# A merged issue list, dealt buffer places and five idle products in a spectral and GLU kernel

## The chip, the cores and the metric

The kernel runs on one core of one Trainium2 chip. The time is device microseconds of one execution. Three executions of the kernel before took 1094.29, 1090.46 and 1092.93 us; their median is 1092.93 us. Engines are named as in the profile: PE multiplies matrices, DVE, ACT and POOL work on vectors, SP issues DMAs (POOL and ACT issue some too).

## The reference

Four layers act in turn on x of 2048 rows and 512 columns, in fp32. A is a filter in the spectrum, B is a bilinear gated unit; each works on the normalised x and is added to x.

```python
def _A_ref(x, w_r, w_i):
    X = jnp.fft.rfft2(x, axes=(-2, -1))
    X = X * (w_r + 1j * w_i)
    return jnp.fft.irfft2(X, s=(S, D), axes=(-2, -1))

def _B_ref(x, w_gate, w_up, w_down):     # 512 -> 1792 -> 512
    h = (x @ w_gate) * (x @ w_up)
    return h @ w_down

x = A_x
x = x + _A_ref(_layernorm(x), A_w_r, A_w_i)
x = x + _B_ref(_layernorm(x), B_w_gate, B_w_up, B_w_down)
x = x + _A_ref(_layernorm(x), A_w_r, A_w_i)
x = x + _B_ref(_layernorm(x), B_w_gate, B_w_up, B_w_down)
```

The output is x after the four.

## The kernel before, in words

**Tiling and stages.** x lives in SBUF as `xs`, 16 tiles of 128 rows by 512. The kernel calls an A with the B behind it a layer; there are two, and each runs through these stages.

- *Forward*, 16 tiles t (`fwd`, `fwd_rest`): statistics of the row, a scale by the reciprocal deviation put into a twiddle factor `tw`, for some tiles a fold `fo` on POOL, four products into a bank `tp` ("spread"), and copies or sums into `E`, which holds the spectrum.
- *Middle*, 16 groups g (`middle`): sums `fs` on DVE for g = 0 and 1 and on POOL for the others, sixteen small products into `dp` ("features"), a copy `zs` on ACT, a product `zp` by the constant `midt`, the filter on DVE into `ys`, products into `vq`, and a copy back into `E`. The first group needs all 16 forward tiles.
- *Inverse*, tiles t (`inv`): products `yi`, a copy or sum `vs`, a product `yo`, added to `xs`; then the statistics for B. Half the tiles run here, the other half between the first units.
- *Transposes* (`build_x`, and for the second half of the tiles `stage_x` and `unstage_x` through memory, with `zt`): the normalised tile `xn` is turned (`tq`) and split in a high and a low part, `XA` and `XS`.
- *Units* (`unit`): seven products of blocks (`gw`, `gx`, `gy`, `gz`, `gv`) with sums on DVE (`q`, `q5`, `c22`) and a copy `s1` on ACT in between, so that the gate and up products take seven instead of eight block products. The names s, q and c in the profile are `s1`, `q` or `q5`, and `c22`. Then the down products: plain (`db`) for the first and the last, in between in seven products again (`down`: `ex` to `ev`), whose left sides `sf` are made by ACT and POOL and whose right sides `bf` are fetched from memory by a DMA that POOL issues (`load_forms`). Every product of fp32 numbers is three products of fp32r parts (`mm3`).

**The order of the work.** Nothing is issued when it is written down. Each step is recorded by `plan.op` with its engine, what it reads (`r`) and what it writes (`w`); from these follow the steps that must stand before it. `Plan.order` then reads a list written into the kernel, `ORDER`: the compressed differences of the step numbers, 4939 of them. The steps are issued in that order, and `Queue.call` keeps every engine's instructions in program order, so the list sets the order on each engine. That call is line 296, and so all lines of the profile carry L296; its groups are told apart by their tiles.

**Rings.** Most tiles take a place in a ring, a set of buffers of one size: `x`, `y`, `w` (one bank of PSUM each), `a` (three), `d` (two), `f` (eleven of 128 by 512 in SBUF), and smaller ones for twiddles, statistics and the forms `sf`. `bank` and `temp` ask for a tile with the ring's name as its tag and the ring's size as its number of buffers, and the framework deals the place. A new tile waits until the last instruction that uses the former tile of its place has ended. For the forms (`slot`) `order` works out the place itself, as the one that was free for longest.

**At the start of each middle stage**, the last spreads, their copies into `E`, the first `fs` and the first features follow one another; in layer 0 that is near 27 us, in layer 1 near 573 us.

Of the kernel before, what the change touches and what calls it, by code (L numbers as in the profile page):

```python
# [11 lines left out]
F32 = mybir.dt.float32  # L12
# [16 lines left out]
def consts():  # L29
# [74 lines left out]
FAST = (0, 1)  # L104
FAHEAD, BOFF, COFF, IOFF, W1, HPDUE, TOFF = 2.79, 9.0, 6.0, 5.0, 10.0, 40.0, 6.0
# [29 lines left out]
    'Q`oVGf<F#0a$Q(2!7I(Mb2mHuDtXPx|Nq+=+9sGswG~nMmRQA-uYGh8_cnyOV3OL(Ch0%m&xv8hrO;<BgBM)DPkS`dD_k$<Iz{fI!nt4(2JdCEGSmXOZ~(Qz19B5Bx{@hh=GR)e6kjBZ'
    '>B_(98)(~D8&WaNMSDk~Mi@tgT}$0&zg`dOdoiB5pZ3{UXLV&m-6!@TzQEf?sm=B0v@!jY%nn~6FX82tSX~NbIXSF;oK&P%n;mRFq7TU%?ALQ*S?q#Z?OBQ)8zb+^&H6gE<3ReE8ng=K'
    'Bi7c7$QUG_f&8cO$fe}#++g1|SRVxxd=E;B$?bj7I5+d%pL_QbQH}^)tWETFv>aY#tm$&r-_Nf|CZMa5<VSj$RbF4F#pA^8bauNiU?No#dpS`jNh{d!xu7rx1S=vL2JTy;e>dp_btt>f'
    'sZ^beCy)1~K5?kJf-v${YKW_XI<U&?a$PKK^kVlF3Oa&aB9v8uHVXbUjWIvy&Qip2d9>eUpwCG!)?<D=K}?%PpZE-Cp2^imgLhMCS-@H%IZt+PNj~fV7gg3=(3%vYzj;{4#YE>4l)a7d'
    'c)0U=P$pI{JxjiPg3kbuHD5RBSysD^-V4Z5E#T1wp#CRcS=tgqsnQ$YZKG{s+!gvADsd7hnj?2IdWJ0XWATXX-wHK7pY5AEQyGTj0#@ciBn=4q^*dJeIr|%-j7<4=W>1d5rklcwEAqRK'
    'JPA9T;CD4@GS$gcZ0)el5Z5v==~(=0nz1E)pE8w3z4d^5(%&qmi6*1Go~QTc<n)2AIsWR6*9+l=F6hf=c)EyHu2j>aUEthD*_S@j)W7IVIh+N5U$Y9s$Uthu0$3<3>|83=7*<M$$Y{;3'  # L140
    'tt7v!)t*lM1+C@g_#W~Tb2RgBxw0X4o+aw4h7*qKSW|oXHYj{UN$KE|eBz=EHRSG4`|i-^X>UI22ygW8-(veteOz{iTs^~?5=tm4v(3Dbgoms6_E80_-bsCF9P=3Yxns11{Ff6vpAN6R'
    'MIWzQ8T&E*F2`GuWcr5DH?aIRyzg0;ja3LrpP_Cwm3ev4k#?el{$r(Aur}i%W8=l_N=<h3O8iradq3hYL-RcLuNRS15YE<mp_1(c;g?YB=7$rWoqXGA9GN&SA9Vns^VM+EiCw)8TwI3+'
    'JrK8#`pF0JIjt78#ClupXRP4c_<oeiAXsN>Si1)UUCD#Su_;(TkKQ}+Xz7GvgE{KJ7>D(f_~z(8@z`h^_tLnxgTEEn=^X4_5<iL>t4D9Iuf%<$h4Fx>JQ1>0n+ML0;H@WgkItokVouA{'
    'wR!ech{bE*jmP3?(IGXhvIHCriOVKUB<nZFht<eu4aj-F=;!!m11OI1$~?UYU)udlJ~csXS+T2#h%LZ_j_(|PH7&^-KfsN7VYUXW^N8LZuVu$=uh-Eki<$O;<r-pVhbvrHe?sepr^(cC'
    'J(zJdYQa?Q5!ysxcpKJL3~Hiz(2s@S#H)Q<2LBBm{v8NBfrUG$DJ?FKf!!*>nnF!vvKk?_?ToZmH~~Bz@Ysks8neGAiIIfjE)P4{&fB?XKNuql_j?mzso{*a4tX`3zX#PcR(jw&J10DZ'
    'uhuZuAAG9e$=b3^t(L67NOt0NnErLbcM(Xhf~DnY`w#TtNo<`52cHDNCt>?F`htwmcVMQ&L{B=SX0Xl*0SD>)U61zd#Yi_0ojWygV)h9r8$k~{yX(N}4ro)j_5dTNgXX3vigfxf)60S`'
# [54 lines left out]
class Plan:  # L201
# [36 lines left out]
    def order(self):  # L238
# [5 lines left out]
        for o in ops:  # L244
            for t in o["tiles"]:
                t.left, t.slot = t.users, None
# [21 lines left out]
def kernel(ctx: ExitStack, tc: tile.TileContext, x, wf, wc, wb, dfwd, tf, ti, mid, out):  # L268
# [679 lines left out]
    ws = {}  # L948
# [167 lines left out]
```

## Time and profile before

| | |
|---|---|
| median of three executions | 1092.93 us |
| the profiled execution | 1092.97 us |
| its span, first to last instruction | 1091.2 us |
| mean granted clock of PE | 0.991 |
| PE busy | 1059.6 us (97%), 6536 products |
| DVE busy | 817.0 us (75%) |
| POOL busy | 752.8 us (69%) |
| ACT busy | 404.2 us (37%) |

The table has the profiled execution beside the median of the others. Busy times are sums over the span; the rest of an engine's span is idle. PE is the engine that is seldom idle, so what matters is where it waits, and how fast it is allowed to run: the granted clock is 1.00 for nearly all of the span and 0.50 in a few stretches. In the timeline, a row has the start, the duration, the engine, the operation with its tiles (output, then inputs), the shape and the count; the bracket at its end is the time for which the engine was idle before it, and the instruction that ended that time. In the windows, each engine has its busy time and a count of instructions in brackets, and PEclk is the clock that was granted to PE.

### The profile page before, as it was taken

How to read it: one execution, taken by the hardware profiler on the slowest of the kernel's cores; microseconds unless marked ns; L12 is line 12 of the kernel's file. 1: busy time of each engine (PE TensorE's matmuls, PEld its weight loads, DVE VectorE, ACT ScalarE, POOL GpSimd, SP SyncE). 2: the span in 40 equal slices, each digit the busy share in tenths (PEclk: the TensorE clock that was granted, in tenths of full speed). 3: DMA queues.
4: the chain of work that ended last, by engine and by line, in shares of the span. 5: the costliest groups of instructions: out<-in, count | busy, mean ns of one | idle time of the engine just before them, and what ended most of it. 6: DMA issues, size and time to landing. Idle time of an engine off the chain costs nothing.

```text
span 1091.2 us, 18622 instructions
## 1 busy us (share of the span) xinstructions
PE 1059.6 (97%) x6536; PEld 912.2 (84%) x6536; DVE 817.0 (75%) x1603; ACT 404.2 (37%) x965; POOL 752.8 (69%) x1000
## 2 busy tenths in 40 slices
PE   8999999999899999999989999999999999999998
PEld 6676888888699988889976679888889998888887
DVE  7776867778777567777896768768888876667688
ACT  6456643333343322232354466123233422222321
POOL 6746698998899746757746328465578984656772
PEclk9999999999999999999998999999999999999999
DMA  9512545778663566547381001646778247555642
GB/s 354 222 44 108 173 174 202 244 243 284 191 218 139 203 202 205 182 149 229 123 323 71 1 18 58 213 153 194 224 241 261 78 138 245 187 189 195 206 135 78
DMA packets 84668, 193.65 MB, mean 177 GB/s; under 512 B 39264, under 2 KB 50784, under 8 KB 73568
## 3 DMA queue, kind: packets, MB, share of 16 engines
q0 software_dynamic: 16128, 102.77, 28.4%
q1 hardware_dynamic: 68160, 89.18, 24.3%
q8 instruction: 52, 0.85, 0.3%
q10 hardware_dynamic: 288, 0.52, 0.1%
q14 instruction: 40, 0.33, 0.1%
HBM read 145.52 MB, written 46.92 MB: 176 GB/s over the span
## 4 chain that ended last, share of the span: by engine, by line
PE 81%; DVE 7%; POOL 5%; ACT 2%; issue 1%; DMA 1%; DVEq 0%; POOLq 0%; ACTq 0%
PE gz L296 13%; PE gx L296 13%; PE gy L296 6%; PE gw L296 6%; PE gv L296 6%; PE db L296 6%; PE ex L296 5%; PE ez L296 5%; PE dp L296 3%; PE zp L296 3%; PE ew L296 3%; PE ey L296 3%; PE ev L296 2%; PE yi L296 2%; DVE xs L296 2%; PE vq L296 2%
## 5 line engine op out<-in xcount | busy, mean ns | idle before, releaser
L296 PE MATMUL gx<-xA,wt 128*128 128x512 f32 (+1 forms) x852 | 181.9, 349 | 4.1 <-ACT s L296 2.6
L296 PEld LDWEIGHTS gx<-xA,wt 128*128 128x128 f32 x852 | 138.3, 191 | 23.3 <-ACT s L296 3.2
L296 POOL TENSOR_TENSOR sf<-cc,sf 128x256 fp32r<-128x256 f32 x97 | 71.5, 739 | 48.6 <-ACT sf L296 47.3
L296 DVE TENSOR_TENSOR xs<-xs,db 128x512 f32<-128x512 f32 x128 | 85.1, 680 | 20.1 <-PE db L296 19.7
L296 POOL TENSOR_TENSOR sf<-q,sf 128x256 fp32r<-128x256 f32 x101 | 74.3, 739 | 34.5 <-ACT sf L296 31.0
L296 PE MATMUL db<-wd,h 128*128 128x512 f32 x336 | 91.6, 399 | 0.6 <-DVE xA L296 0.6
L296 PE MATMUL gy<-xS,wt 128*128 128x512 f32 (+1 forms) x426 | 90.7, 348 | 1.2 <-ACT xS L296 0.6
L296 PE MATMUL gz<-xA,wt 128*128 128x512 f32 (+1 forms) x426 | 90.7, 349 | 0.2 <-DVE c L296 0.2
L296 PE MATMUL gz<-xS,wt 128*128 128x512 f32 (+1 forms) x426 | 89.8, 347 | 0.7 <-DVE q L296 0.7
L296 PE MATMUL gv<-xS,wt 128*128 128x512 f32 (+1 forms) x426 | 90.0, 347 | 0.0
L296 PE MATMUL gw<-xS,wt 128*128 128x512 f32 (+1 forms) x426 | 89.9, 347 | 0.0
L296 ACT COPY s<-gx 128x512 f32<-128x512 f32 (+1 forms) x71 | 35.1, 495 | 144.2 <-PE gx L296 131.1
L296 PEld LDWEIGHTS gy<-xS,wt 128*128 128x128 f32 x426 | 69.0, 190 | 11.0 <-POOL xS L296 0.9
L296 PEld LDWEIGHTS gw<-xS,wt 128*128 128x128 f32 x426 | 69.4, 190 | 10.1 <-DVE q L296 0.4
L296 PEld LDWEIGHTS gz<-xS,wt 128*128 128x128 f32 x426 | 68.9, 190 | 10.3 <-DVE q L296 1.1
L296 PEld LDWEIGHTS gz<-xA,wt 128*128 128x128 f32 x426 | 68.8, 190 | 10.3 <-DVE c L296 0.9
L296 PEld LDWEIGHTS gv<-xS,wt 128*128 128x128 f32 x426 | 68.9, 190 | 9.3 <-issue 0.5
L296 POOL TENSOR_TENSOR wt<-rg,wt 128x512 fp32r<-128x512 f32 (+1 forms) x56 | 64.0, 1154 | 13.9 <-ACT wt L296 13.8
L296 PEld LDWEIGHTS db<-wd,h 128*128 128x128 f32 x336 | 61.4, 189 | 14.3 <-issue 3.2
L296 DVE TENSOR_TENSOR q<-gy,s 128x512 f32<-128x512 f32 (+1 forms) x71 | 40.9, 577 | 39.2 <-PE gy L296 23.4
L296 ACT CAST sf<-q 128x256 fp32r<-128x256 f32 x101 | 40.8, 406 | 72.5 <-DVE q L296 31.6
L296 PE MATMUL ex<-bf,sf 128*128 128x256 f32 x408 | 60.4, 285 | 1.2 <-DMA bf<-dn 1.2
(161 smaller groups left out, 2532.4 us busy)
## 6 DMA issues: line engine op xcount, KB each, us to landing
wt<-gu POOLq DMA_DIRECT2D x36, 1024.0 KB, 5.4
wt<-gu POOLq DMA_DIRECT2D x36, 768.0 KB, 5.1
bf<-dn POOLq DMA_DIRECT2D x20, 1024.0 KB, 5.5
wq<-in_wf_dram SPq DMA_DIRECT2D x16, 1024.0 KB, 10.9
bf<-dn POOLq DMA_DIRECT2D x20, 768.0 KB, 4.7
gu<-wt SPq DMA_DIRECT2D x14, 1024.0 KB, 5.8
gu<-wt SPq DMA_DIRECT2D x14, 768.0 KB, 5.1
rg<-in_wb_dram SPq DMA_DIRECT2D x14, 512.0 KB, 4.2
```

Source lines behind the costliest of these rows:

```text
L296: ins = f(*args, **kw)
```

## The change

- `ORDER` is a new list of 4944 steps. It was merged in order of the times that are expected for the steps.
- Every place of a ring is now a buffer of its own: its tag is the ring's name and a digit, and it has one buffer. The digit is read from a string, `PLACES`, which has 2328 hexadecimal digits, one for each tile in a ring in the order in which the list first uses them. The rings keep their sizes. `order` no longer works out any place.
- `keep_warm` records idle products ahead of the middle stage: two in layer 0, three in layer 1. Each is one product of 128 by 512 of the constant `midt` with itself into a new tile `wp` in bank `w`, which nothing reads. The key `"idle"`, written by the spread of the last tile (t = 15) and by the idle products and by the first features (g = 0), puts them in this order: last spread, idle products, first features.

```diff
+IDLE = 2, 3
 ORDER = (
-    ...
+    ...
+PLACES = (
+    ...
@@ class Tile_
-        self.users = self.left = 0
-        self.freed = 0.0
+        self.users, self.placed = 0, False
         self.index = 0
         self.tile = None
+
+    def tag(self):
+        return f"{self.ring}{self.index}"
@@ Plan.order
-        ops, rings, done = self.ops, {}, set()
-        turn = np.cumsum(steps.astype(int))
+        ops, done = self.ops, set()
+        turn, places = np.cumsum(steps.astype(int)), iter("".join(PLACES))
         assert sorted(turn) == list(range(len(ops)))
-        for o in ops:
-            for t in o["tiles"]:
-                t.left, t.slot = t.users, None
-        for n, i in enumerate(turn):
-            o = ops[i]
-            assert o["pre"] <= done
+        for i in turn:
+            assert ops[i]["pre"] <= done
             done.add(int(i))
-            for t in o["tiles"]:
-                if t.slot is None:
-                    t.slot = True
-                    q = rings.setdefault(t.ring, [])
-                    t.index = len(q)
-                    if len(q) == self.RINGS.get(t.ring, 1):
-                        old = min((u for u in q if not u.left), key=lambda u: u.freed)
-                        t.index = old.index
-                        q.remove(old)
-                    q.append(t)
-            for t in o["tiles"]:
-                t.left -= 1
-                t.freed = n
+            for t in ops[i]["tiles"]:
+                if not t.placed:
+                    t.placed, t.index = True, int(next(places), 16)
         return [ops[i] for i in turn]
@@ bank, temp
-        return Tile_(name, tag, lambda: pp.tile([128, 512], F32, name=name, tag=tag, bufs=NB[tag]))
+        t = Tile_(name, tag, lambda: pp.tile([128, 512], F32, name=name, tag=t.tag(), bufs=1))
+        return t
...
-        return Tile_(name, tag, lambda: wk.tile(list(shape), dt, name=name, tag=tag, bufs=NB.get(tag, 1)))
+        t = Tile_(name, tag, lambda: wk.tile(list(shape), dt, name=name, tag=t.tag(), bufs=1))
+        return t
@@ fwd_rest
-        pe(0.9, spread, [*src, tw], [tp])
+        pe(0.9, spread, [*src, tw], [tp, *(["idle"] if t == 15 else [])])
@@
+    def keep_warm(n):
+        for i in range(n):
+            bk = bank("wp", "w")
+            pe(0.86, lambda bk=bk: TE.matmul(bk(), midt[:, 0:128], midt, start=True, stop=True), ["midt"], [bk, "idle"])
@@ middle
-        pe(0.83, features, [(fs, 0), (fs, 1), df], [dp])
+        pe(0.83, features, [(fs, 0), (fs, 1), df, *(["idle"] if g == 0 else [])], [dp])
@@ the loop over the layers
         dcs["i"] = load_di()
+        keep_warm(IDLE[layer])
         for g in range(16):
             middle(g, E, dcs["f"], W, t0 + BOFF + BSTEP * g, SWAPS[layer][g])
```

More of the change, by code (lines that the diff above doesn't have):

```diff
@@ new lines @@
+    '<w4$>uES&(y^7Ogofg5*g##b%WS$pfk+xv$!#rQCCuIUriY8(gS!;1gWt0j*|Ie}Ts=go#iF%4YBXgOlIUXs@O8UuC?JH{;VYrTvjy!u=RxwXanWJ-cy!_2ti{jZF;!=@VMDpGkd=Vy-'
+    'S$_>?36n|siMVy$(~-Pgk$6?aKT)z%XW*^k@`^6`*Q)YZenTBf?r8$H4AFU#$=H!nOnT^ixrQB~c)tWFzoyOcVHnSgGor&=CUzH<r-)C4xE@_}C#~r^P*+HaAR`J&3tc9qiDV9|GxD@t'
+    'u?n&-N_|<bO>|e#k|E`_h$$+q%`bi_bJdnITlGo2(+k{&%MwuDM3(8Jyb~@N_JVvW&thQ>y&y^EjIAeA)W^>~<qx8mLBE<>*rejgNkk(~zQ^Wr8fKCiGZ_yK2HPF+)D$pVPE(0@x`xO;'
+    '(9%^_fSY|}nUQB$wdxw($JkA!EODzZZ*$#3R-15}U(;m1OtM*;VBD(S)B^mjNe12LtqRy4g3S@c`W$Fz#MR^AEmk(^er;@`^fI=j5&=)1k`F+7L+KzRwHi;FV|BJplr?1JYcfq+;{SK`'
@@ new lines @@
+    'aXBMH^j)6r!h0UMmQTh=6+BU%(N&Xmi5`bjX6hh$p1dC;N!s6hX)noE)>xUgu~M1$zR@=DLsPCQgQtV?8Ch(}=`&=;dELdEugWm#6WmpzR~UHjOHTE{mO0v$XwT7ab%Tr{_Yd-O1O#jY'
+    'eMfYUz62^3X?ND%m-oI0+dFi-Ow<u(t(^&0j65OxOkdkiJ^^j{WwQ>I!#Y}KgXDTxGMo|f%h&Qce05Z}>QgYs%hF5}$@XlWjtyl&*H^53xJ+dY<;cj%`ig0%9hk8=a~fi*<Wr1%N|xS%'
+    'Nfz49W}jZQCCnWn@<76|B1`W3L^gkz-@vbIdJvg@QVf16C@Ogx31i)cqjEub1YRh{xOZ6jcM^luj?avom6D+B3|Emnzol2DxZaS8MAM^h7*8U}n=IP8!M>-Zs>JJJo;Q@Gj8ei}v5{sE'
+    'mKGs4`QSYxe@Y{A%~ciAl4dUvOC`_Kh{0JcqGioFdRKNe2VM*}S$dYaDye7AXay`PB!}@u8JMw}oaV`Ma?0j6=WQi(-=@I$?svFekxF><7@63V9F8X!Lb3fZ*rlua7^XO7|1yQN9HaDQ'
@@ new lines @@
+    '-Fx7}IiT-vJxv}S#d~R5MIXVo8q}OhuxpAw3-=t*npz7xLiILW(i}9jBr+#qoK$;I`hwnB+8@83wDnCMqf}yLw|Npx#QxMFAmDdab{GG<igAg|{L)5><-H1W+;%X|C+juS_AwXmK}Bjw'
+    'EKj!K8CTCzK!=gpww!587NoP9J#h4LZ7Zd~%rff5cKf<Hs=LXkY2YkB78Qki7wI#2?=lsk8M9v33mQkfvg|GT*E8@OSH(2MC?oE(*O{v}<1fP7x%fYqoV$RBp2K%Zc&Rze(@lP6<rcdP'
+    '4E{8|e_}<u$=n#K_bmEUk?*vXB!c(H$=@_$l>wrv!9LGY^=8<eW)Ys)3U6)29s>&1dh)V4#a##DdWH(Kff~AtIm$6=y8gus>D;C9-exk}p(395&d|1*k$c*`W)-z8m0av;J@3PyPg6XT'
+    'tqtwRW|Tc^uEWcPseBh<fkzp2AwD{!pV=Qxe)uq54^q(w;O|a$nz^NKS-8bqgfpIH?Hz51cMjg^0?Qra_ph`X-uW9(_mUict?6Lrk?{q*ba=0uElBSNx&x-T1drC%*QLG9F@KY7b-`sc'
@@ new lines @@
+    'N-2$OZ7*f*2@_-Ud3XJB*qo32S;uNDKTdU2mUKTy&zU6ZSy^!zlI45MTTp6wtMwJT&BPOr$`WNSnzMc@$tPc#o)YQ3?oYKLjPSl`%{m{Uwmi(SlOX-H-_6_0OegetZ@zz&6||COGMe$@'
+    '!G0V_9c1sB^?o-wXEu@%b3x5~oe8EQ><IIL6k_Dz=9hp+7s6B{sWWGE7I>c^tNb)A?IlPxnc?Sh^&F$k)KBFLKi*66U-Rbrjl501k(a%1{d`_?d~+VOu7qp$Q^(3;mD7P|u=NaROvZ!F'
+    'si&L#1TT$Bwafp=d&4j0J@9LI#iSGHS}Co}CI2pMW4UW8seTOeT-Wm^Ru1}K(A$&t-a2OV^>c59=C?bvmFMBN4`qzsT<+o7vHr8(CI6yH_q%&>GRq(2z3or-R9Aw(^ZL8r&#Ob`Uf^zl'
+    '-@|)Vn)z*|9b-m$7ySy}FaD=^`z!CD{^T34f$i@l!&p^hp6{}`rX+atSo;J2r1tWT`D)^b;WJW4+WYIg(>g~##O@dIevC9lH@5McvXXYeyVJZO{H=x#7~{RJ1?(X2XPto6(O!y%+dREz'
@@ new lines @@
+    's>%ibhQ8p1VVMEx9lVv~XiK!sRs5O{Zk!#|yT<Y>ez{MC8j$(vT3_Dv-}8!siZy;`R$?{AJL@<0+K}I&sEBR4-k;zZkn;nT=^&Wdh0PuC<xsB*b^o%S$7eNQfyPwW7s>GXy3k+g{RL+|'
+    'VCJe=f13FdsdO>YLVh83Jx$%bS>9G{jV?Y(o<_n<7hw37@N=Z>hpA)HPP@T!X*i)aSj>PYQv(()LpA&ZJ#vmdam2*!368_+u`sq9v7|idU)DulG`>2)Xr%%zRgO$*#pqFTk&KOF#!Rqv'
+    '0F;!$%BzfA3R}vN+a1Iy^)ghY0$lkh^V`%sMIlFt``Ls2+oU=fa)r5%gUsL6mo|*BQQYpp*Qa4upX#(yp44#PdMBxbUG-pIfshz@tUD2@MLleu7aFpe_Ef2=OW|!F{t09L&RAWSoWI4a'
+    '_w#O%KbO!r{is+su{adZ=BL`vHv2W#jsh!#q^a&BCvWO|SkRdazDk_)gMchO#Qi14DT=KJq>Jvzs}vH=NcZrI)m2n!XYrQ2>LKOvURl}}OC0&OKCf-aB6%9M+!TFz9&J~RwY`J7xP)gi'
@@ new lines @@
+    '_;FfnIQ92K{eYd|9GKyK^8YkDwfovbdSTCL9fcL+K>we51XfH9#`qJzWCs;Jm8&Q;^jG3gSww!5MRv1H;mzV9oAUCsPsj&(BVYrxn{)&lwXn2>%%EpQ^weCm<`eLsv)=~FP>JOMuJf~s'
+    '6S`LZ@Mh=DlKf~9)#0dF4_!Key-gRqQJ?s<mC-UxKSR;ogIPX9$xe~S!B3i;u{&8;6KPM|AG!rwhoWT@(0V(iIUL@T)w^h|(%JI2b#0z(4=k9i-?0~YQQY6!K}!f&ZHUHsj=6HsjGxJC'
+    '{Qevp4Wmy({jSx)%$|?gR)e_Lbg&G;!rN5%be?=ENwQI2!b^#?mgPQ?abwtLc*JwL)RlHHq#I`nnfx^o3nGd-SPGIHnl|Yy`47lx$BrZxPrr_e$q6*rw{p|I6I^#@jjMFE-iBp<q=qj+'
+    'xin^^R$9?~&rUKksKAMg?0$RLJRNH-ckOwzBRjTixMmF+W?!&3nnFtv@bj1%M&v?R?L<7P>iB#TckiJ&jr7NV${wJqbf#{6EFY6MpMsdvaLFn>UzeFW^Ya@jKZ%`cXOOl8ERCj5Z>?%J'
@@ new lines @@
+    'P@`+&-*NEHTH=+9MTPm@72TAeXT@pR(%QtVP<Mt<OEYO{Cj+Ht5Q#AA+=f8a-qINT8^+xXPh2zY?LNItblS*eTN(uwkN?{e`wwIUYk4H_Zxr}Rg+ty&(cfXE3E<&?x}DM?H2eu-e~w+_'
+    'IGJa|jZ;YHv3jJuPs>E`x5;Kp7xrNuYH<Zms|OL8z?>toW-<)4f=Cqu16}@&rbFlnMt&Mb>dhXo8&Qn_RqL^|7kL+kjx=OrNT9=uVEYRE>e`CHxQ9VtGJJB_4mTcGS>R;|ib(bUS62^K'
+    'cdN71*mbZ&16Gm~_-z{eIUY~0v>%#d#N;^R-w9SzR2JCh%m}Ww+U=$VdO*=%t6<mm*s(g`*`w-wQWtzqB!=tt4ZL$5o_8aCLL}D*=N&DHvD<BQ1X*3kc{gt;9=M4OMNlkPxN9z_z*aW*'
+    'Em=`*=?zotVk9b){lOFwhcdU~&)G4bge?vSGv8z_9c`{IFpq+sZ04FIZ{f{)JS!ykvG5ca%A<<ih4)Ory>6sq+S%UJ?S|USiV8?gyTH^yo3}<u6!tFQxh}-*Q|)X@%J=pyM)(@mJ+3WL'
@@ new lines @@
+    '2URA5UDawL(3r6Y>Q<QyXF4BD#zRT?b~P3xvEMp^FPG8MDQG)@%{R47u$D1YrC6+VYd4H`gw?E6cgo|=eH>!P1YgBR2TE)_N^DH<{qiX2bAHN)ids*tSPSQLBO+8-GN~-}s0H<@NsxVo'
+    '8Q<x@zwx`Pd8^r9Te!F=d%qpQ|Gw$Q7&$>S9t7uwIl+$5{hz9a>;>Hp(9Pw})jKd^Ztz9Kol_TP+=Aq~tB6~)2WxziTwR9uZ|T<Hdrky6>l#$YF7R7Tap#=w1am2RraoMDgId!FYqH?3'
+    'G-4lx{<s3h+-b;B`jldZ>%kdAML05=sHCX-@*6{j=VGf>_kU~(i~A<>D6w(>5AA;e&)2jE')
+PLACES = (
+    '0000000000000000000000001230045670001110121232130305400014650574001906160a0817000170000111015102032610090700850406002113900a8007065003920114'
+    '0030060a0011902000a054030010907501000008290010a100020050a0003712090800001100040702000500310260a209070102011801232045036310a02903110615002910'
+    '0110042a000501612495050a420600084002150a00802196000011200000500100200105573100000041a800070100100000020040001160008100710000263a011480101100'
+    '0070418070910000a010000040010a084610106070101a0100000a1104000180a00700200100510071090a5001210001000080607011002920a1410840160106001180003400'
+    '1a00420012011900801160100027100042519601005091050070101710000000a0106140010501174091000061003071040000101001601000a1000071001001350060001120'
+    '07201a05110060100700002133000012000a036140000503000011000001a9006015230203007400081a90600124005000812a0903110340702180a001490107a40123041050'
+    '4006000001024050300013504600011210144002040a8002000001021040400035210a04000071003a0110200150400217004211501003190430002110040523040800300600'
+    '4142920038012011402061a500080413210004001090081311700408090012141000182500712010090520831040200111052001602330600004021010a10040681300210001'
+    'a0205004412130100300849110100528030007030100119440050110a1020060031660211014001152002114000111013200150770a707300201409608060a52000407091183'
+    '062a50800014051037600004500091a306008040030921000146070511040080605000a0001180020240610095000002a011303081520727400121426001292061514a000052'
+    '181030047010302120050030095650a803104017200000162a08157900400000001018103a0070523404010100132070015000022000311094600603007002a0162011603400'
+    '703002040026011030804090030020501160240139103000068100a010010a80240234000811040011007004121381405007001130105618053420010a102703403050111042'
+    '0400008070013910504100000812a31620001908306050a02008a3190464a01000130012033100048741000a04002303812214011060307110703900a6048490201a12093015'
+    '0010a010002290030500481a10309020514901071300040409a120210007310609314002a00070002112340104030080a00215134030a002074120800050000a090000710051'
+    '0802000a709050340000410012003000a00249400010310a004072309120003007040005001207200005813160a2041005713804200010304012000201003502006300910300'
+    '0540040025303012100400180620001310804106230001110020a073080232108010610420005103301010046030125100040116102090410056004300101010652304009001'
+    '8230010400a091081002a30120009134010007201a11051020300214610812001704010a0000091010012100')
```

93 lines of the change are left out of this document (32 added, 61 removed).

## The prediction

> **What bounds the kernel now.** I read the page first (busy times, chain), then the windows of 20 us, then windows of 3.41 us around every change of PEclk, last the timeline at PE's waits.
>
> ```profile
> span 1091.2 us, 18622 instructions
> PE 1059.6 (97%) x6536; PEld 912.2 (84%) x6536; DVE 817.0 (75%) x1603; ACT 404.2 (37%) x965; POOL 752.8 (69%) x1000
> PE 81%; DVE 7%; POOL 5%; ACT 2%; issue 1%; DMA 1%; DVEq 0%; POOLq 0%; ACTq 0%
> ```
>
> The profiled execution took 1092.97, so 1.8 lie outside its span; the median of the runs is 1092.93, the same within 0.04, and the sum is made against 1092.97. PE is busy for 97%, and idle for 1091.2 − 1059.6 = 31.6 us. Nothing here removes a product, so time can come from two places only: those 31.6 us, and products that run at half clock.
>
> Windows (PE, PEld, DVE, ACT, POOL busy, then PEclk, DMA share, GB/s):
>
> ```profile
> 26.81:30.22 3.41, 1.80 (x21) 1.35 (x23) 2.90 (x4) 0.58 (x1) 3.41 (x5) 1.00 1.01 414
> 30.22:33.64 3.42, 3.42 (x20) 2.26 (x16) 0.00 (x0) 0.58 (x1) 2.79 (x5) 0.50 1.01 417
> 40.00:60.00 20.00, 20.00 (x175) 14.43 (x175) 16.87 (x25) 11.30 (x21) 14.94 (x22) 1.00 0.10 40
> 98.49:101.90 3.41, 1.16 (x5) 0.30 (x4) 2.98 (x8) 2.17 (x6) 0.81 (x2) 1.00 0.01 2
> 293.05:296.46 3.41, 2.83 (x7) 2.26 (x8) 2.29 (x4) 2.79 (x5) 1.59 (x2) 0.50 0.17 25
> 463.72:467.13 3.41, 2.06 (x10) 1.37 (x9) 1.64 (x3) 1.27 (x3) 3.31 (x6) 1.00 0.75 216
> 569.53:572.94 3.41, 0.47 (x5) 0.28 (x3) 3.31 (x10) 0.37 (x1) 1.24 (x2) 1.00 1.00 423
> 572.94:579.77 6.83, 5.96 (x38) 4.46 (x40) 1.21 (x3) 1.17 (x2) 5.51 (x10) 0.50 0.78 278
> 600.00:620.00 20.00, 20.00 (x180) 14.90 (x176) 16.03 (x25) 10.33 (x19) 8.75 (x11) 1.00 0.00 1
> ```
>
> After a 3.41 us stretch in which PE was busy for 1.80, the next runs at PEclk 0.50; after 0.47 two do; after 2.06 (463.72:467.13) none did. Both middle stages (40:60, 600:620) have PE at 20.00 of 20, so what is saved at their start is not given back to a later wait inside them.
>
> **The change, part by part. 1: five idle products.** Two stand between the last spread of layer 0 and the first features of its middle stage, three in layer 1.
>
> ```profile
> 16.78 0.33 SPq L296 DMA_DIRECT2D midt<-in_mid_dram  x1
> 27.18 0.44 PE L296 MATMUL dp<-df,fs 128*64 128x128 f32 x2 [1.75 <-DVE fs L296]
> 29.95 1.77 PE L296 MATMUL dp<-df,fs 128*64 128x128 f32 x16 [0.82 <-ACT zs L296]
> 31.65 2.07 PE L296 MATMUL zp<-zs,midt 128*128 128x256 f32 x4
> 567.83 3.73 DVE L296 TENSOR_TENSOR E<-tp,tb 128x256 f32<-128x256 f32 x11
> 573.04 1.98 PE L296 MATMUL dp<-df,fs 128*64 128x128 f32 x16 [3.04 <-issue]
> 575.79 1.97 PE L296 MATMUL dp<-df,fs 128*64 128x128 f32 x16 [0.77 <-ACT zs L296]
> 577.69 2.08 PE L296 MATMUL zp<-zs,midt 128*128 128x256 f32 x4
> 616.59 1.10 PE L296 MATMUL dp<-df,fs 128*64 128x128 f32 x16
> 617.62 1.13 PE L296 MATMUL zp<-zs,midt 128*128 128x512 f32 x2
> 632.33 1.02 PE L296 MATMUL yo<-vs,tw 128*128 128x512 f32 x2
> 633.19 1.89 PE L296 MATMUL yi<-di,E 128*128 128x256 f32 x8
> ```
>
> A product of this shape holds PE for 633.19 − 632.33 = 0.86. Two, 1.72, fit the gap of 1.75 ahead of 27.18; three, 2.58, fit the 3.04 ahead of 573.04: added on the path, nothing. Without these gaps as cover they would cost 5 × 0.86 = 4.3. What they bring is the clock. Groups that took 1.77 and 2.07 took 1.10 and 1.13 at full clock: 0.67 + 0.94 = 1.61 in layer 0. In layer 1: (1.98 − 1.10) + (1.97 − 1.10) + (2.08 − 1.13) = 2.70. Together **4.3**. Behind an idle product that waits stand the first features and all of PE. It waits for midt, issued at 16.78 and read by 31.65 in any case: a late landing takes back at most layer 0's 1.61 plus the wait, and the new list puts the load ahead of three loads that stood before it on SP. In layer 1 it waits for bank w, below. Layer 0 is the tighter: only 27.18 − 26.81 = 0.37 of the gap lies in the stretch ahead of the cold one, so its 1.80 becomes about 2.2, near the 2.06 that held. In layer 1 0.47 becomes about 3.0.
>
> The Trainium skill, page "TensorE: Matmul & The Clock Gate", section "Part 1: The HAM clock gate", gives half clock after an idle window of about 3.4 us, and its section "HAM oscillation" says to avoid idle gaps of more than that. By it a gap of 1.75 would halve nothing, and the sum would lose 1.6; the row disagrees, since 1.80 of busy was enough to halve the next stretch.
>
> **2: places dealt out.** I wrote both lists out by their operations and compared who held a place before. A new tenant waits for the last reader of the old one.
>
> ```profile
> 271.88 1.53 PE L296 MATMUL gx<-xA,wt 128*128 128x512 f32 x6
> 277.64 0.69 DVE L296 TENSOR_TENSOR q<-gy,s 128x512 f32<-128x512 f32 x1 [3.23 <-POOL h L296]
> 278.39 1.65 PE L296 MATMUL gz<-xS,wt 128*128 128x512 f32 x6 [0.67 <-DVE q L296]
> 286.51 0.69 DVE L296 TENSOR_TENSOR q<-gz,c 128x512 f32<-128x512 f32 x1
> 291.42 1.46 DVE L296 STREAM_TRANSPOSE zt<-xn 128x512 f32<-128x512 f32 x2 [2.04 <-POOL h L296]
> 292.99 0.58 ACT L296 COPY s<-gx 128x512 f32<-128x512 f32 x1 [2.97 <-DVE zt L296]
> 293.63 2.93 PE L296 MATMUL gx<-xA,wt 128*128 128x512 f32 x6 [2.57 <-ACT s L296]
> 458.67 0.69 DVE L296 TENSOR_TENSOR ew<-ez,v 128x512 f32<-128x512 f32 x1
> 465.49 0.69 DVE L296 TENSOR_TENSOR cc<-gx,q 128x512 f32<-128x512 f32 x1 [1.98 <-POOL sf L296]
> 466.24 0.96 PE L296 MATMUL gx<-xA,wt 128*128 128x512 f32 x3 [1.35 <-DVE cc L296]
> ```
>
> At 292.99 the copy s takes a place of ring f from an xn that zt reads until 292.88. In the new string its predecessor is c22, read last at 286.51 + 0.69 = 287.20: the wait of ACT goes, and PE's 2.57 with it. The product itself took 2.93 at PEclk 0.50 (window 293.05) against 1.53: 1.40 more. At 465.49 cc follows s2, which POOL still reads; its new predecessor is a v, read last at 458.67 + 0.69 = 459.36: 1.35 go. At 277.64 q follows a q that POOL's h reads; its new predecessor is a yb of the second half's inverse, whose readers come earlier: 0.67 go. Sum 2.57 + 1.40 + 1.35 + 0.67 = **6.0**. What is late next: s, cc and q then wait only for their own products, which are the instructions just ahead on PE; bounds 0 (another wait ends last) to 6.0. I take 6.0, by the row at 271.88, where the same gx group has no gap ahead of it and takes 1.53.
>
> **3: the merged list.** Five idle products aside, nothing is added or removed: against the old sequence 367 of 1120 PE entries, 1087 of 1602 DVE, 636 of 936 ACT, 768 of 995 POOL and 241 of 284 SP stand elsewhere, most PE ones by a place or two. Two places can be read from rows.
>
> ```profile
> 99.73 1.14 ACT L296 COPY sx<-tq 128x512 f32<-128x512 f32 x3 [1.52 <-DVE xA L296]
> 101.00 1.54 ACT L296 ACTIVATE xn<-xs,rs 128x512 f32<-128x512 f32 x2
> 101.90 1.12 PE L296 MATMUL tq<-ident,xn 128*128 128x128 f32 x4 [2.26 <-ACT xn L296]
> 883.79 1.86 POOL L296 TENSOR_TENSOR xA<-xf,xA 128x768 fp32r<-128x768 f32 x1
> 885.59 0.57 POOL L296 DMA_DIRECT2D bf<-dn  x1
> 892.57 0.95 PE L296 MATMUL ex<-bf,sf 128*128 128x256 f32 x6 [1.23 <-DMA bf<-dn]
> ```
>
> ACT's copy sx waited 1.52 for DVE's xA; the new list has that copy ahead of the xA copy, so the wait goes, and with it up to 1.52 of PE's 2.26. The stretch before (98.49, busy 1.16) halved the clock of the next; if that goes too, up to 1.12 + 1.14 more, by half of the later groups. Bounds 0 to about 4; I take **2.0**, near the row of ACT. At 892.57 ex waits 1.23 for a fetch that POOL issued at 885.59, behind the piece xA of 1.86; the new list has the fetch ahead of it, and 1.86 is over 1.23: **1.2**. The piece xA starts later by the fetch's 0.57 on POOL; I count nothing for it, and 0.57 if a product waits for it.
>
> For all the other moved entries no row gives a price. An engine works in order, so an entry put too early holds all behind it. By the nearest rows one such wait in a dense stretch cost 2.57 + 1.40 = 4.0; the upper end is several of these, the lower end what idle time is left: 31.6 − (2.57 + 1.35 + 0.67 + 2.26 + 1.23) − (1.75 + 3.04) = 18.7, of which I count half, since a change of stage must wait for something: −9. I take **+3**, most of one such wait: hundreds of entries moved, but hardly any PE entry far.
>
> Sum: 4.3 + 6.0 + 2.0 + 1.2 = 13.5 gained, 3 lost: 1092.97 − 10.5 = **1082.5**.
>
> **The rivals.** *Idle products only* (13 in 100): the ring waits leave one place and come up at another, the list gains as much as it loses; 1092.97 − 4.3 = 1088.7. For it: idle on PE is spread over stage changes, where several engines end close together. *Layer 0's products don't hold the clock* (9 in 100): 2.2 against 2.06 is close, and a stretch that begins elsewhere has another share of the gap; 1082.5 + 1.6 = 1084.1. It is also what the Trainium skill's rule, named above, comes to. *Nothing* (10 in 100): three products in layer 1 wait for bank w. DVE's sums E end 567.83 + 3.73 = 571.56; if the last tile were in w, the products would end at 571.56 + 2.58 = 574.14, 1.1 after the 573.04 of before, and the order's gains go into its losses: about 1092. Against it: the new list has t = 14, the one in w, ahead of 11 and 15. *Slower* (16 in 100): places dealt by expected times are tight. If the last reader of a place runs late on the chip, the new tenant holds DVE or ACT in order, and PE behind them, in the dense units, 4.0 each time as at 293. With all gains (1092.97 − 13.5 = 1079.5) it takes more than (1096.2 − 1079.5) / 4.0 = 4.2 such places to end slower; five give 1099.5. For it: DVE has 1087 entries elsewhere, and the old rule dealt by last use. Against: before shows only the three ring waits of part 2 that held PE for over half a microsecond.
>
> **How the numbers follow.** The forecast 1082.5 has 52 in 100, from 1074 (1082.5 − 9) to 1089; with the others 13, 9, 10, 16. About 0.3% is what a measurement can tell here, so same is 1089.65 to 1096.2. Faster: 52 + 9 + 7 (half of idle products only, which lies near the bound) = 68; same: 6 + 10 = 16; slower: 16. The range from 1074 to 1096 leaves out the slower case and the ends.
>
> **What would show it.** Right: PEclk 1.00 in the stretches that now begin at about 30 and 573, dp groups of 1.1 there, a product wp in the gaps; no wait of over 1 us at s near 290 and cc near 462; PE idle near 23. Wrong: new gaps on PE in the units whose releaser is POOL or ACT with a ring tile; PE idle unchanged at 31 or more; wp waiting for DVE E.

## The result and the profile after

The changed kernel took 1081.6 us (median of four, 1080.65 to 1083.88) beside 1092.83 for the kernel before (four, 1090.46 to 1094.29). The ratio is 0.9902, with a 95% interval of 0.9879 to 0.9926: 11.2 us less by the medians. The profiled execution took 1080.65. Executions of one kernel differ with the clock that they were granted: of 22 of the kernel before, one of 1095.25 us had a mean of 0.989 and one of 1090.23 us a mean of 0.994.

From the page of the changed kernel: its span, the busy times, and the chain that ended last by engine.

```profile
span 1078.9 us, 18673 instructions
PE 1054.7 (98%) x6546; PEld 900.9 (84%) x6546; DVE 817.1 (76%) x1603; ACT 406.5 (38%) x965; POOL 752.2 (70%) x1000
PE 80%; POOL 6%; DVE 5%; DMA 2%; issue 2%; ACT 2%; SPq 0%; DVEq 0%; POOLq 0%; ACTq 0%
```

PE's idle time fell from 31.6 to 1078.9 − 1054.7 = 24.2, its busy time from 1059.6 to 1054.7, with ten more instructions. So 7.4 of the gain is waiting and 4.9 is busy time. The 4.9 is a net figure. In before's trace PE ran at half speed for six steps of 3.41 us (from 30.22, 101.90, 293.05, two from 572.94, and from 627.56); the changed kernel's trace has no such step ahead of its last 1.4 us. Against that stand the idle products (2.21 + 3.39); the pace of the products changed too, with both signs (experiment 9).

The timeline of the changed kernel at the places of the prediction's steps, in order of time (the group of wp is two and three idle products; each counts two instructions).

```profile
25.73 2.21 PE L307 MATMUL wp<-midt 128*128 128x512 f32 x4
27.86 0.43 PE L307 MATMUL dp<-df,fs 128*64 128x128 f32 x2
30.36 1.10 PE L307 MATMUL dp<-df,fs 128*64 128x128 f32 x16 [0.77 <-ACT zs L307]
98.75 0.63 PE L307 MATMUL tq<-ident,xn 128*128 128x128 f32 x4 [0.27 <-ACT sx L307]
284.14 0.56 ACT L307 COPY s<-gx 128x512 f32<-128x512 f32 x1
454.05 0.69 DVE L307 TENSOR_TENSOR cc<-gx,q 128x512 f32<-128x512 f32 x1
559.89 3.39 PE L307 MATMUL wp<-midt 128*128 128x512 f32 x6
564.05 1.10 PE L307 MATMUL dp<-df,fs 128*64 128x128 f32 x16 [0.77 <-issue]
565.92 1.10 PE L307 MATMUL dp<-df,fs 128*64 128x128 f32 x16 [0.77 <-ACT zs L307]
780.65 0.59 ACT L307 COPY s<-gx 128x512 f32<-128x512 f32 x1 [5.02 <-DMA turns<-zt]
781.29 1.67 PE L307 MATMUL gx<-xA,wt 128*128 128x512 f32 x6 [2.26 <-ACT s L307]
827.72 0.42 DVE L307 TENSOR_TENSOR q<-gy,s 128x256 f32<-128x256 f32 x1 [2.16 <-DMA xf<-turns]
828.20 0.97 PE L307 MATMUL gz<-xS,wt 128*128 128x256 f32 x6 [1.12 <-DVE q L307]
880.74 0.88 PE L307 MATMUL ex<-bf,sf 128*128 128x256 f32 x6
```

The groups dp take 1.10 where before took 1.77 and 1.97. The copy s at 284.14, the sum cc at 454.05 and ex at 880.74 carry no bracket: they wait for nothing. And there are two gaps that before did not have, at 781.29 and 828.20: PE waits there for ACT's s and for DVE's q, whose own releasers read "DMA".

Where the time went is best read as a ledger. Each product was matched with itself in both traces; the difference of its two starts is the lead at that point. The table has the change of the lead over stretches of the kernel before.

| stretch of before, us | changed kernel − before, us | what lies there |
|---|---|---|
| 0 to 96 | −1.2 | start (+0.4), idle products of layer 0 (−1.6) |
| 96 to 146 | −5.4 | inverse, transposes and first units of layer 0 |
| 146 to 265 | +2.7 | units of layer 0, no gap on PE on either side |
| 265 to 312 | −5.4 | q at 277 and s at 293 |
| 312 to 515 | −1.8 | cc at 465 (−1.5) |
| 515 to 600 | −0.5 | +0.6, then layer 1's idle products (−1.0) |
| 600 to 665 | −3.0 | end of layer 1's middle stage, inverse, first units |
| 665 to 870 | +4.5 | the two gaps above, and smaller ones |
| 870 to 1074 | −1.8 | fetch of bf (−1.8 by 912), then nothing |

Together −11.9 by 1074; the two profiled executions differ by 1092.97 − 1080.65 = 12.3. Part of it belongs to the execution and not to the change: the half-speed steps behind 293 (1.4) and 627 (1.7) are missing from the traces of experiments 1 and 3 too, which keep before's list.

### The profile page after: what moved, and what is told of

It is laid out like the page before. It is cut to its first block, busy times and chain, and to the rows that moved or that the text cites. A ratio compares the mean times of both kernels' runs of the same rounds, so it can differ in the third digit from the quotient of the medians.

```text
span 1078.9 us, 18673 instructions
## 1 busy us (share of the span) xinstructions
PE 1054.7 (98%) x6546; PEld 900.9 (84%) x6546; DVE 817.1 (76%) x1603; ACT 406.5 (38%) x965; POOL 752.2 (70%) x1000
## 4 chain that ended last, share of the span: by engine, by line
PE 80%; POOL 6%; DVE 5%; DMA 2%; issue 2%; ACT 2%; SPq 0%; DVEq 0%; POOLq 0%; ACTq 0%
PE gx L307 13%; PE gz L307 12%; PE gw L307 6%; PE gy L307 6%; PE gv L307 6%; PE db L307 5%; PE ex L307 5%; PE ez L307 4%; PE dp L307 3%; PE yi L307 3%; PE zp L307 3%; PE ev L307 2%; PE ew L307 2%; PE ey L307 2%; PE vq L307 2%; PE yo L307 2%
## 5 line engine op out<-in xcount | busy, mean ns | idle before, releaser
L307 PEld LDWEIGHTS gx<-xA,wt 128*128 128x128 f32 x852 | 136.0, 188 | 21.9 <-ACT s L307 2.5
L307 POOL TENSOR_TENSOR sf<-cc,sf 128x256 fp32r<-128x256 f32 x103 | 75.9, 740 | 24.7 <-ACT sf L307 24.3
L307 POOL TENSOR_TENSOR sf<-q,sf 128x256 fp32r<-128x256 f32 x89 | 65.6, 739 | 32.4 <-ACT sf L307 31.8
L307 ACT CAST sf<-q 128x256 fp32r<-128x256 f32 x89 | 36.2, 406 | 87.2 <-DVE q L307 35.5
L307 POOL DMA_DIRECT2D wt<-gu x72 | 40.5, 563 | 35.5 <-PE gw L307 22.4
```

Source lines behind the costliest of these rows:

```text
L307: ins = f(*args, **kw)
```

## The experiments

Ratios are to the kernel before, run on the same chip. "Own buffers" means that each place of a ring is a buffer with a tag of its own.

**1. Idle products alone.** The kernel before, with `keep_warm` and its key, list otherwise kept.

```diff
         dcs["i"] = load_di()
+        keep_warm(IDLE[layer])
         for g in range(16):
```

> The kernel before with the five idle products alone: same list, same ring places. Theory (the clock is what they bring): layer 0 gains about 1.6 us (dp and zp groups of 1.1 in place of 1.77 and 2.07). In layer 1 the last spread, t = 14, stands in bank w, which is drained near 571.5, so three products of 1.1 end near 574.9, 1.9 after the 573.04 of before, against 2.7 gained: 0.8 net. Together 2.4 faster than before. Rival, the clock was not what they bring: no gain in layer 0 and 1.9 lost in layer 1, about 2 slower than before.

Measured: 1090.1 us, ratio 0.9978 (0.9969 to 0.9988): 2.3 faster. Layer 1 in this kernel, by timeline and by windows cut at the steps of the clock (PE, PEld, DVE, ACT, POOL busy, PEclk, DMA share, GB/s):

```profile
569.24 5.05 PE L297 MATMUL wp<-midt 128*128 128x512 f32 x6 [1.70 <-DVE E L297]
574.22 1.10 PE L297 MATMUL dp<-df,fs 128*64 128x128 f32 x16
```

```profile
567.13:570.54 3.41, 1.65 (x7) 0.66 (x6) 3.31 (x9) 0.37 (x1) 1.30 (x2) 1.00 1.01 425
570.54:573.95 3.41, 3.35 (x4) 0.75 (x4) 1.15 (x2) 0.00 (x0) 3.41 (x7) 0.50 1.02 404
```

With before's list the products wait 1.70 for bank w, which DVE's sums still read, as the rival "Nothing" described it. Then the half speed falls on the idle products themselves, 5.05 in place of 3.39, and the features behind run at full speed. Layer 0 gained 1.6 in this trace and layer 1 lost 0.9; the rest of the 3.0 between the two traces is steps of half speed that this one does not have behind 293 and 627. So the total and layer 0's part are as expected, layer 1's is not, and the total is partly chance.

**2. The changed kernel without idle products.**

```diff
-IDLE = 2, 3
+IDLE = 0, 0
```

> The changed kernel without its five idle products; list and places as changed. Theory: the stretches after the two gaps run at half clock again, 1.6 and 2.7 lost, and 0.9 of products beyond the gap of layer 0 and some of layer 1 regained: 2.5 to 4 slower than the changed kernel's 1081.6, so about 1084 to 1086. Rival, the changed order alone keeps the stretches busy enough: 1081 or less.

Measured: 1085.67 us, ratio 0.9936 (0.992 to 0.9952), 4.1 slower than the changed kernel by the medians, 3.7 by the ratios. Timeline and windows of layer 1:

```profile
562.73 1.98 PE L307 MATMUL dp<-df,fs 128*64 128x128 f32 x16 [3.99 <-issue]
```

```profile
557.50:560.88 3.38, 1.23 (x12) 1.04 (x10) 3.23 (x11) 0.74 (x2) 0.11 (x1) 1.00 1.01 422
560.88:571.12 10.24, 7.63 (x52) 5.96 (x52) 4.99 (x7) 1.17 (x2) 7.09 (x11) 0.50 0.28 95
```

The gap of 3.99 leaves PE 1.23 busy in a stretch, and the next three, 10.24 us, run at half speed. With the new list layer 1's products are worth 3.5 in the trace (+2.5 in 556 to 600 here, −1.0 with them). In layer 0 this execution had no half speed, and came out 1.1 earlier without the products.

**3. Addresses alone.** The kernel before with each engine's order and each tile's place as they were dealt, but own buffers; the places are written in `PLACES`, and there are no idle products.

```diff
-        return Tile_(..., tag=tag, bufs=NB.get(tag, 1)))
+        t = Tile_(..., tag=t.tag(), bufs=1))
```

> The kernel before with every engine's order and every tile's place as the framework dealt them, but each place a buffer of its own, so that only addresses in memory change; no idle products. Theory (a place costs by who held it, not by how it is declared): the time of before, 1092.8 within 3. Rival, the layout itself sets the pace of the products: in the changed kernel a product of six 128x512 takes 1.40 where before took 1.36 to 1.39; were that from buffers of their own, up to 287 x 0.03 = 8 us slower than before.

Measured: 1091.31 us, ratio 0.9989 (0.9978 to 0.9999). That is the time of before within 0.3%; by the interval own buffers bring 2.4 us at most by themselves. But 146 to 265 took 1.5 longer than in before without any new gap. At 293 the same wait stands, and the windows, cut at the steps of this trace's clock, divide it:

```profile
295.11 1.66 PE L305 MATMUL gx<-xA,wt 128*128 128x512 f32 x6 [2.48 <-ACT s L305]
```

```profile
290.11:293.52 3.41, 2.53 (x11) 1.71 (x10) 1.38 (x4) 1.32 (x2) 2.93 (x4) 1.00 0.17 62
293.52:296.93 3.41, 1.82 (x8) 1.51 (x9) 2.51 (x5) 2.46 (x5) 0.61 (x2) 1.00 0.12 19
296.93:300.35 3.42, 3.42 (x17) 2.74 (x16) 3.27 (x6) 0.40 (x1) 3.39 (x4) 1.00 0.52 77
```

In before one step holds the whole gap:

```profile
289.64:293.05 3.41, 1.42 (x7) 0.84 (x5) 1.60 (x3) 0.44 (x2) 1.97 (x2) 1.00 0.00 0
```

The gap is that of before (2.48 beside 2.57), yet nothing runs at half speed behind it: the product takes 1.66, not 2.93. Here two steps share the gap, with 2.53 and 1.82 us of busy time; in before one step had 1.42, and the next ran at 0.50.

**4. Three other places in the old list.** Kernel 3, and q near 277, zt near 291 and s near 293 take places whose former tenants were read earlier (all later tenants of the two places change with them).

```diff
-PLACES: q 0, zt 5, s1 3
+PLACES: q 3, zt 9, s1 6
```

> The kernel before with its order and its dealt places, each place a buffer of its own, and three tiles of ring f given another place near 277 to 293: q takes the place of a vs, zt that of a u2, s1 that of a u2. No idle products. Theory (these waits are what a place costs): the gaps of 0.67 and 2.57 on PE go; against the kernel with own buffers and no other place (1091.3) 3.2 faster, and 1.4 more in executions in which the gap would have halved the clock: about 1087.5. Rival, another wait (q behind DVE's transposes) ends as late: 1091.

Measured: 1086.93 us, ratio 0.9953 (0.9941 to 0.9965); 4.4 faster than kernel 3 by the medians, 3.9 by the ratios, whose intervals do not meet. PE at the place of the former gap:

```profile
289.87 1.56 PE L305 MATMUL db<-wd,h 128*128 128x512 f32 x6
291.26 1.53 PE L305 MATMUL gx<-xA,wt 128*128 128x512 f32 x6
```

No bracket is left, and 4.1 of the difference between the two traces lies between 265 and 312. Three tiles at other places are worth 4 us: it was the place, and nothing else ended late there.

**5. The new list, places dealt by the framework.** The kernel before with `keep_warm` and the new `ORDER`.

> The new list with the idle products, but the places dealt by the framework as before. Theory (dealt places are worth 6.0): 1081.6 + 6 = about 1087.6, with gaps of 1 to 3 us on PE behind ring tiles near 290 and 460. Rival, the list alone makes the gain and the places none: 1081.6. Second rival, the string loses by places whose last reader is a store of zt (PE's gaps of 2.26 near 781 and 1.12 near 828 in the changed kernel), and the framework's dealing avoids them: 1078.

Measured: 1088.96 us, ratio 0.9964 (0.9951 to 0.9977), 7.4 slower than the changed kernel by the medians, 6.8 by the ratios. The total is as the theory said, but the gaps are not where it put them. PE near before's 293, with no bracket (nor is there one near 277 or 465):

```profile
292.28 1.56 PE L299 MATMUL gx<-xA,wt 128*128 128x512 f32 x6
```

The loss against the changed kernel lies between 170 and 270, at three other points: 2.8 near 173, 0.5 near 193, and 2.4 near 264 with 1.4 of half speed behind it.

```profile
166.92 0.37 ACT L299 COPY yb<-yi 128x256 f32<-128x256 f32 x1 [4.14 <-DMA dn<-u]
172.37 1.66 PE L299 MATMUL gz<-xS,wt 128*128 128x512 f32 x6 [1.03 <-DVE q L299]
173.85 0.69 DVE L299 TENSOR_TENSOR q<-gw,q 128x512 f32<-128x512 f32 x1 [1.54 <-POOL u L299]
175.28 0.93 PE L299 MATMUL db<-wd,h 128*128 128x512 f32 x3 [1.26 <-DVE rs L299]
264.51 2.26 PE L299 MATMUL db<-wd,h 128*128 128x512 f32 x6 [2.17 <-DVE xs L299]
```

ACT's copy yb waits 4.14 for the place of a u2, a piece of the down weights that a store to memory still reads. ACT's later steps are late with it, among them the s that DVE's next q, and PE's gz behind it, need. The q at 173.85 takes its place from an rw, a piece of weights that POOL is still turning into a u2. In the changed kernel the same yb, at 163.62, waits for nothing. The wait near 264 was not followed to a place. And 96 to 146 is 5.4 shorter than in before, as in the changed kernel: that gain is the list's, with either kind of places.

**6. Two tiles off the places of zt.** The changed kernel; s near 781 and q near 828 take other places.

```diff
-PLACES: s1 a, q 2
+PLACES: s1 6, q 5
```

> The changed kernel with two tiles of ring f given another place: s1 near 781 takes that of an s2 and q near 828 that of a v, both in place of a zt that a store to memory reads. Theory (a place that was last read by a DMA is free only when that has landed): PE's gaps of 2.26 and 1.12 go, 3.4 faster than the changed kernel, about 1078. Rival, ACT and DVE were late there anyway: 1081.6.

Measured: 1078.82 us, ratio 0.9881 (0.9867 to 0.9895), 2.8 less than the changed kernel by the medians, 2.3 by the ratios; the intervals overlap, the rows do not:

```profile
777.39 0.87 PE L307 MATMUL ez<-bf,sf 128*128 128x256 f32 x6
778.10 1.55 PE L307 MATMUL gx<-xA,wt 128*128 128x512 f32 x6
```

```profile
822.56 0.43 DVE L307 TENSOR_TENSOR q<-gy,s 128x256 f32<-128x256 f32 x1 [0.29 <-PE gy L307]
```

PE goes from ez to gx without a gap, and q waits for its own product. But only the first of the two is a gain: the trace gains 2.5 on the changed kernel's near 781, and the 1.3 that it gains near 828 are lost again by 840, where PE waits for POOL three times, among them:

```profile
832.39 0.74 PE L307 MATMUL ev<-bf,sf 128*128 128x256 f32 x4 [0.41 <-POOL sf L307]
```

**7 and 8. Other offsets.** The changed kernel with unused bytes in memory (the tile shown, of 16 columns or 24, and larger statistics tiles), so that the operands of the units begin at 96, or at 0, modulo 128 bytes (as changed: xA, xS, h, wd at 32, wt at 96; before: all at 96).

```diff
     hp = cp.tile([128, 2, 32], F32, name="hp")
+    cp.tile([128, 16], F32, name="gap")
```

> The changed kernel with 64 unused bytes ahead of its ring tiles and larger statistics tiles, so that the operands of the unit products (XA, XS, wt, and h, wd, sf) start at 96 modulo 128 bytes, as in the kernel before; in the changed kernel X, h and wd start at 32 and wt at 96. Theory (this offset sets the pace, not the list): a product of six 128x512 takes 1.36 to 1.38 in place of 1.399 (275 of them, 7 us less), one of six 128x256 takes 0.716 in place of 0.703 (442, 6 us more): 1081 within 2. Rival, the list sets the pace: 1.399 and 0.703 as in the changed kernel.

> The same with other sizes of the unused bytes, so that all these operands start at 0 modulo 128 bytes. Theory (equal offsets of both operands matter): paces as with all at 96, 1.37 and 0.716. Rival (the offset itself matters): another pace, up to 10 us either way, since 0.02 of 275 + 442 products is 14 us.

Measured: 1081.77 us, ratio 0.9914 (0.9899 to 0.9928), and 1084.85 us, ratio 0.9931 (0.9917 to 0.9944). The pace is the distance from one product's start to the next one's, as a mean over all gx to gv and ex to ev of six products each (275 of 128x512, 442 of 128x256). It was 1.393 and 0.714 in both, where the changed kernel has 1.399 and 0.703. So it moved, but before's 1.36 to 1.38 did not come back: the theory of the offset fell. Kernel 8 is 3.1 slower than kernel 7 by the medians; the intervals overlap, and the pace does not explain it.

**9. The old addresses.** Kernel 6 with every place at exactly the address that it had in before: the first tile of each is asked for in before's order of addresses, ahead of the list.

```diff
                     t.placed, t.index = True, int(next(places), 16)
+                    first.setdefault(t.tag(), t)
+        for tag in LAYOUT:
+            first[tag]()
```

> The kernel whose two tiles were moved off the places of zt (1078.8), with every ring place at exactly the address that it has in the kernel before; list, places and idle products are kept. Theory (addresses alone set the pace): six 128x512 in 1.36 to 1.38 in place of 1.399, six 128x256 in 0.717 in place of 0.703, and the 146 to 265 stretch of before regains its 2.7: 1079 within 1.5. Rival (the sequence of the products sets it): 1.39 to 1.40 as with the other addresses, and the stretch stays 2.4 to 2.7 longer.

Measured: 1077.76 us, ratio 0.9865 (0.9848 to 0.9882). The pace in the three kernels, PE in a stretch of layer 0 with no gap; the time from one row to the next is the product of the first. Before:

```profile
172.19 1.52 PE L296 MATMUL gw<-xS,wt 128*128 128x512 f32 x6
173.55 1.52 PE L296 MATMUL gx<-xA,wt 128*128 128x512 f32 x6
```

The changed kernel:

```profile
173.97 1.56 PE L307 MATMUL gx<-xA,wt 128*128 128x512 f32 x6
175.37 1.56 PE L307 MATMUL gv<-xS,wt 128*128 128x512 f32 x6
```

The changed list at the old addresses:

```profile
173.44 1.53 PE L311 MATMUL gx<-xA,wt 128*128 128x512 f32 x6
174.81 1.52 PE L311 MATMUL gv<-xS,wt 128*128 128x512 f32 x6
```

1.36, 1.40 and 1.37, all at PEclk 1.00 and with no gap. In the last kernel 146 to 265 is 0.07 longer than in before, where the changed one is 2.7 longer. So the addresses set the pace, and the list does not. Over the whole kernel it nearly cancels: six 128x512 take 1.374 on average in place of 1.399, but six 128x256 0.717 in place of 0.703.

**10 and 11. Fewer and more idle products**, in kernel 6.

```diff
-IDLE = 2, 3
+IDLE = 0, 3     # and, in the other, 4, 6
```

> The kernel with two tiles moved (1078.8), without the two idle products of layer 0. Theory (what they bring hangs on where the stretches of 3.41 us begin; they hold the first features back by about 0.7 to 1.1 in every execution): between 1 faster and 2 slower, 1079 in the middle. Rival, they hold the clock in every execution: 1.6 slower, 1080.4.

> The kernel with two tiles moved (1078.8), with twice as many idle products, four and six. Theory (the gaps are full with two and three): each further product of 1.07 to 1.13 holds the first features back; five of them, less the 0.77 left near 564 and the 0.2 near 28: 4.5 slower, about 1083. Rival, half of them still find cover: 1081.

Measured: 1080.22 us, ratio 0.9889 (0.9874 to 0.9904), not to be told from kernel 6; and 1086.25 us, ratio 0.9949 (0.9936 to 0.9962), 7.4 slower. Without layer 0's products the first features start 0.9 earlier than in kernel 6 and run at full speed in this trace; a later gap is followed by half speed here:

```profile
74.20:77.61 3.41, 1.58 (x12) 1.22 (x11) 1.57 (x3) 1.25 (x4) 0.00 (x0) 1.00 0.70 228
77.61:81.02 3.41, 3.26 (x8) 2.63 (x9) 0.00 (x0) 0.92 (x3) 2.64 (x3) 0.50 0.00 0
```

With four and six:

```profile
25.60 4.58 PE L307 MATMUL wp<-midt 128*128 128x512 f32 x8
30.10 1.10 PE L307 MATMUL dp<-df,fs 128*64 128x128 f32 x16
561.12 6.94 PE L307 MATMUL wp<-midt 128*128 128x512 f32 x12
567.99 1.10 PE L307 MATMUL dp<-df,fs 128*64 128x128 f32 x16
```

The features come right behind the products. From the first product to the features it is 4.50 and 6.87, beside 2.13 and 4.16 in the changed kernel: 2.4 + 2.7 = 5.1 more. The trace with four and six has two steps of half speed, from 619.37 and 841.24, that kernel 6's trace does not have, but it is also 10.8 longer than that; how much of the further 2.3 between the medians they are is open.

## Why the prediction was right

The time (1082.5 forecast, 1081.6 measured) and its two sources, waits and half speed, were right. The terms were less right than their sum.

- **Idle products, 4.3.** The mechanism holds in layer 1: 3.5 in the trace with the new list, and dp at 1.10 in place of 1.97. A product was mis-sized: 1.07 to 1.13, from (27.86 − 25.73) / 2 and 3.39 / 3, not 0.86; three of them filled the gap in layer 1, and two pushed layer 0's features back by 1.1. Layer 0's 1.61 is what experiment 1 shows, but experiment 10 could not separate it from nothing. The rival "Layer 0's products don't hold the clock" named the reason: which stretch is slow depends on where the stretches begin. They began at 30.22 in before, at 30.69 in experiment 3 and at 27.65 in experiment 4, and experiment 3 has the gap of 293 without its half speed. The Trainium skill, page "TensorE: Matmul & The Clock Gate", section "Part 1: The HAM clock gate", says that the window runs freely; that agrees. That a whole idle window is needed does not agree with these rows: 1.42, 1.65, 1.23 and 1.58 us of busy time in some 3.4 were each followed by half speed.
- **Places, 6.0.** A wait does hang on who held the place before, and the size came out near; which waits the string removes was wrong. The step counted the three waits at 277, 293 and 465 for the string. Experiment 4 shows that other places remove the first two in the old list (4.4, or 3.9 by the ratios). But experiment 5 has the new list without the string, and none of the three is there either. So the 5.4 between 265 and 312 and the 1.5 at 465 in the ledger come with the list alone: experiment 5's trace gains 5.2 and 1.6 there. What the string is worth under the new list, 7.4 (6.8 by the ratios), are waits near 173, 193 and 264, which the new list has with the framework's places and which the prediction did not look for. That this is near 6.0 is luck. And the 1.40 for half speed is not the place's own, since it goes in some executions anyway.
- **Merged list, 2.0 and 1.2.** The fetch gave 1.8. The stretch at 100 was under-sized: the list gave 5.4 between 96 and 146, and experiment 5 shows the same with the framework's places. PE's wait ahead of tq fell from 2.26 to 0.27 (98.75), and no half speed followed; the bound of 4 was too low, because before's later gaps at 110.48, 111.29 and 128.44 (0.61, 0.42 and 0.65) closed too. Half speed can have cost there 1.7 at most, half of a step of 3.41, and not 1.12 + 1.14. A gain of 3.0 between 600 and 665 was not in the sum; 1.7 of it, at 618 to 645, is half speed that experiment 3 lacks too, with before's list. That the three waits of the places' term go as well was not counted for the list.
- **All other entries, +3.** Mis-sized: about 8 (2.7 + 0.6 + 4.5 in the ledger). Of that, the gaps at 781 and 828 are the mechanism of the rival "Slower", a place whose last reader is late, at two places and not five, and for a reader that was not thought of: a store that lands after SP issued it. They are also the new gap behind a ring tile that the prediction named as a sign of being wrong. The 2.7 has a cause that no step contained, the addresses.

So an under-sized gain of the list (3 to 5, without the three waits) met an under-sized loss (5). The range held for the reason that it was given, several unknowns of a few microseconds with both signs; the hit within 1 us is luck in good part.

## What to carry to other kernels

Where buffers are dealt from a ring, look for who read the place last: a tile on the critical path should follow one whose last reader is a quick engine and long done, and never one that a store to memory still reads. Experiments 4 and 6 took 4.4 and 2.8 us by moving three tiles and two. A new order deals new places, so the waits that a list of places removes have to be looked for under the order that it comes with. Filler products to hold the clock paid here where the gap was 3.99 us, longer than a step of 3.41 (3.5 in the trace); where it was 1.2 (ahead of 26.87 in experiment 2) they could not be told from nothing. Their own length has to be read from a row that is not overlapped.

The version at hand that beats both is the changed list with two tiles moved: 1078.82, and 1077.76 at the old addresses, against 1081.6 and 1092.8.

## What the runs showed of the hardware

- The pace of TensorE in a gapless run of products depends on where the operands lie in memory: 1.361 or 1.399 for six 128x512 in layer 0, 0.703 to 0.717 for six 128x256, at a granted clock of 1.00, with list and places equal (kernels 6 and 9). It repeats: the changed kernel, its variant without idle products and experiment 5, whose buffers lie elsewhere, all have 1.399. Which property of the addresses does it stays open; the offset in 128 bytes alone does not (experiment 7 has all at 96 as before, and 1.393).
- Half speed comes in steps of 3.41 us that begin elsewhere in each trace (30.22 in before, 30.69 in experiment 3, 27.65 in experiment 4), so the same gap costs in one run and not in the next: 2.57 with 2.93 for the product behind it, 2.48 with 1.66. The busy time of the step before does not settle it alone: behind steps at full speed it followed 0.47 us (569.53 in before) to 1.80 (26.81), and once 2.25 (106.33 in experiment 1), but not the 1.58 at 290.65 in experiment 1, nor the 1.82 in experiment 3.
